# Ordering two sets of small matmuls by an empty GpSimd instruction instead of a TensorE drain, with another step moved between them

## The chip, the cores and the metric

The kernel runs on one core of a Trainium2 chip. The metric is the device time of one execution in microseconds; the time of a kernel is the median of its runs. A core has five engines that work side by side, each through its own queue in order: TensorE (PE in the profile; its weight loads are PEld), VectorE (DVE), ScalarE (ACT), GpSimd (POOL) and SyncE (SP, which here only starts transfers).

## The reference, cut to what matters

The first half is a recurrence per batch and head (4 batches, 8 heads, 768 steps, width 48); its result goes through a small three-way network:

```
cur = einsum('bhd,bhe->bhde', u * kt, vt)
y[:, :, t] = einsum('bhd,bhde->bhe', rt, state + cur)
state = wt[..., None] * state + einsum('bhd,bhe->bhde', kt, vt)
...
h = max(x @ w1, x @ w2, x @ w3);  out = h @ w_out
```

Here x holds y of all heads side by side: 3,072 tokens of 384 values, a hidden width of 768, all in float32.

## The kernel before, in words

The recurrence is worked out in 24 chunks of 128 steps (k = 0 to 23, six for each batch). For a chunk, scores of keys against receptances are a masked 128x128 matrix per head, and the values are taken with it; what came before the chunk enters through a carried state. On TensorE a chunk consists of short blocks of small matmuls, each named by a letter in a table of steps:

- R (`from_state`, L450): reads the carried state into the result y of the chunk.
- X (`scores`, L417): scores of a chunk, here of the next one, k + 1, into two `gram` banks.
- V and Z (`values` and `values2`, L489): two sets of 8 matmuls each that add scores times values into y. Z writes the same banks as V, from the other half of the array's rows.
- U (`to_state`, L460): keys times values for the next state. It uses all 128 rows of the array and is left out in the last chunk of a batch (k = 5, 11, 17, 23).
- T (L437): four transposes. R is left out in the first chunk of a batch.

All float32 matmuls show as two records each, with two weight loads. R, X, V and Z use the array as separate pieces of up to 64 rows and 64 columns; the network's matmuls (L147 and L167), T and U use all rows.

Between V and Z the function `values` puts `nc.tensor.drain()` (L482), an instruction of TensorE's own queue that holds it until the engine is empty.

The step letters stand in strings (`FRONT`, `LAST`, `TURN`, `ORD`); a "|" ends a unit, and units of the recurrence alternate with groups of the network's matmuls by a fixed rule. `ORD` sets chunks 4 to 23: its first unit is R, X of k + 1, V, U, Z, and E (`result`, L503: ScalarE copies y to x), and then b2 and d2, work on chunk k + 2. From chunk 8 on, d is two products on GpSimd (L373 and L374, here called the kr products), whose result VectorE sums into cs in step e (L387, three units later); e also lets GpSimd fill the matrix a with two selects (L393), and then M on VectorE (L426) puts the scores into a. V and Z read a.

Of the kernel before, what the change touches and what calls it, by code (L numbers as in the profile page):

```python
# [40 lines left out]
B, H, S, D = 4, 8, 768, 48  # L41
DM, FF = 384, 768
NP = 4
C = 128
# [7 lines left out]
HC = C // 2  # L52
CPH = HT // C
# [14 lines left out]
FRONT = "n2 w U0 b1 | d1 f1 r1 | w e1 c1 S0 W4 X1 T1 | R0 M0 | V0 Z0 E0 |"  # L68
LAST = "R0 M0 | V0 Z0 E0 n2 w U0 W9 n3 | b1 d1 | f1 r1 w | e1 c1 S0 X1 T1 R1 |"
TURN = "b1 d1 w | f1 w | r1 c1 | e1 M0 w | "  # L70
ORD = "w R0 X1 V0 U0 Z0 E0 b2 d2 | f2 n3 w | S0 r2 c2 | e2 M1 w | T1 w | |"


START = ("aaaaaaaaaaaacaaacaccaxmcacmcamcamcamcamcamcamcamcaamca"
# [16 lines left out]
def kernel(ctx: ExitStack, tc, tin, nat, u_flat, u_pair, v_t, w_all, out, ytr):  # L91
    nc = tc.nc
# [83 lines left out]
    with ExitStack() as fast:  # L176
# [21 lines left out]
        natt = {}  # L198
# [268 lines left out]
        def state(k):  # L467

            if goes_on(k):
                new = prep[k]["pu"][0:112, 0:NP * D].rearrange("p (a b) -> p a b", a=NP)  # L470
                if k % NCH > 0 and k >= CPH:
# [3 lines left out]
                nc.vector.tensor_tensor(out=sstar[(k + 1) % 2][0:112, :, 0:D], in0=new,  # L475
                                        in1=dec[(k + 1) % 2][0:112, :].unsqueeze(2).broadcast_to([112, NP, D]), op=ALU.mult)

        def values(k, second=False):
            p = prep[k]
            fresh = k % NCH == 0 and not second  # L480
            if second:
                nc.tensor.drain()  # L482
            for late in range(2):
                for row in range(2):
                    for half, m in ((0, 64), (1, 48)):
                        hh, j = row ^ second, (1 - row) ^ late
                        h, lo = 4 * half + 2 * j + hh, 64 * row
                        a = p["a"][lo:lo + HC, 2 * hh + half]
                        nc.tensor.matmul(p["y"][64 * half:64 * half + m, hh, j, HC * late:C],  # L489
                                         lhsT=natt[k][0][lo:lo + HC, h * D:h * D + m],  # L490
                                         rhs=a[:, j, :] if late else a[:, j::2 - j, :],
                                         start=fresh and not late, stop=True, skip_group_check=True)

        def values2(k):
            values(k, True)

        def result(k):
# [7 lines left out]
            for lo in (0, 64) if slot == CPH - 1 else ():  # L505
                for j in range(KT):
                    eng = nc.scalar if lo and half < PLAIN else nc.sync
                    eng.dma_start(out=x[lo + 48:lo + 64, j, :], in_=x[lo + 16 * j:lo + 16 * j + 16, KT, :])

        steps = dict(X=scores, M=take, T=transposes, R=from_state, U=to_state, S=state, V=values, Z=values2, E=result, n=load,  # L510
                     b=prep_scan_b, f=prep_scan_f, r=prep_rk, c=prep_check, d=prep_diag1, e=prep_diag2)
        ready = {("n", k) for k in range(3)}
# [16 lines left out]
        def attn():  # L529
            for step in "bdfeWrXTcW":  # L530
                ahead(step, 0) if step != "W" else warmer(2 if ("X", 0) in ready else 8)
            for k in range(NK):
                if k == CPH:
                    nc.scalar.dma_start(out=u_bc[:, :], in_=u_flat.partition_broadcast(128))
                for step in (FRONT if k < CPH - 1 else LAST if k < CPH else TURN + ORD if k == CPH else ORD).split():
                    if step == "|":
# [134 lines left out]
    with tc.If(verdict[0] != 0, label="general"), ExitStack() as slow:  # L671
# [9 lines left out]
        with tc.For_i(0, B) as b:  # L681
            for pr in range(NP):
# [18 lines left out]
                for j in range(KT):  # L701
                    with tc.For_i(0, 16) as i:
# [16 lines left out]
                        for q in range(2):  # L719
                            z = ps_z.tile([2, S // 2], F32, name="z")  # L720
                            nc.tensor.matmul(z[:, :], lhsT=sel[0:112, :], rhs=kv[0:112, q * (S // 2):(q + 1) * (S // 2)],
                                             start=True, stop=True)
                            nc.vector.tensor_copy(out=yo[:, q * (S // 2):(q + 1) * (S // 2)], in_=z[:, :])
                        for hh in range(2):
                            place, lo = 2 * hh + pr % 2, 64 * (pr // 2)
# [8 lines left out]
        for i in range(NW if w_all.dtype != F32 else 0):  # L734
# [3 lines left out]
            lo, hi = words[:, :, 0], words[:, :, 1]  # L738
# [93 lines left out]
```

## Time and profile before

| | |
|---|---|
| median of 3 runs | 424.89 us (424.53 to 431.61) |
| profiled execution, own time | 423.95 us |
| its span | 422.2 us |
| TensorE busy | 408.9 us, 97% of the span |
| VectorE, ScalarE, GpSimd busy | 272.0, 151.9, 74.3 us |
| drains on TensorE | 24, one per chunk |

The span runs from the first to the last instruction of the profiled execution; 1.75 us of its time lie around it. A matmul's end in the trace is modelled from its size, and matmuls overlap, so a block's length is read best from the start of one block to the start of the next.

### The profile page before, as it was taken

Reading aid. Unit: us, or ns where it says so; the run is one execution under the profiler, and the core shown is the slowest. Engines: PE = TensorE matmul, PEld = TensorE weight load, DVE = VectorE, ACT = ScalarE, POOL = GpSimd, SP = SyncE. Lnnn points to the kernel's source line nnn. Section 1 sums busy time; section 2 is a strip of 40 time slices with the busy share of each in tenths; the row PEclk is TensorE's granted clock in tenths of the full one; section 3 lists DMA queues with packets and bytes.
Section 4 is the critical chain, followed back from the end, with each engine's and each line's share of the span. In section 5 each row is a group of like instructions: output and inputs, shape, how many; then the busy total and the mean of one; then the engine's idle time right before and its main releaser. Section 6 shows DMA issues by size and latency. Waiting matters only on the chain.

```text
span 422.2 us, 9012 instructions
## 1 busy us (share of the span) xinstructions
PE 408.9 (97%) x3695; PEld 320.9 (76%) x3695; DVE 272.0 (64%) x515; ACT 151.9 (36%) x318; POOL 74.3 (18%) x92
## 2 busy tenths in 40 slices
PE   6989999999999999999999999999999999999995
PEld 3665545556678888987888988888988888988895
DVE  5988789877769977835867658658547624223320
ACT  1334344232554443424425455334523221312111
POOL 3120111030443140313023113113113100000000
PEclk9989999999999999999999999999999999999999
DMA  8835975244172403295735496653280000200002
GB/s 224 258 100 151 351 250 168 68 168 124 44 231 67 123 7 118 48 283 173 219 92 182 114 279 209 198 180 94 52 265 23 2 2 0 79 18 0 1 2 78
DMA packets 20702, 53.27 MB, mean 126 GB/s; under 512 B 2816, under 2 KB 9088, under 8 KB 20656
## 3 DMA queue, kind: packets, MB, share of 16 engines
q1 hardware_dynamic: 16832, 42.61, 33.3%
q10 hardware_dynamic: 3824, 10.03, 7.6%
q8 instruction: 30, 0.49, 0.5%
q14 instruction: 16, 0.13, 0.1%
HBM read 46.74 MB, written 4.72 MB: 122 GB/s over the span
## 4 chain that ended last, share of the span: by engine, by line
PE 92%; DVE 4%; issue 1%; DMA 1%; ACT 1%; POOL 0%; POOLq 0%; DVEq 0%; ACTq 0%
PE psm L147 55%; PE psm L167 17%; PE y L489 5%; PE gram L417 4%; PE y L450 3%; PE tu L460 3%; PE psm L526 2%; PE tu L437 2%; PE psm L383 1%; DMA out_dram<-m 1%; DVE tin L356 1%; DVE tin L357 1%; DVE gf L345 1%; DVE gf L335 1%; DVE x_lo L107 0%
## 5 line engine op out<-in xcount | busy, mean ns | idle before, releaser
L147 PE MATMUL psm<-x_hi,w 128*128 128x512 f32 x540 | 172.9, 394 | 0.6 <-ACT m L126 0.6
L147 PEld LDWEIGHTS psm<-x_hi,w 128*128 128x128 f32 x540 | 101.4, 188 | 22.5 <-ACT m L126 0.8
L147 PE MATMUL psm<-x_lo,w 128*128 128x512 f32 x270 | 105.3, 390 | 0.0
L129 DVE TENSOR_TENSOR m<-psm,m 128x512 f32<-128x512 f32 x60 | 41.2, 687 | 58.6 <-PE psm L147 52.6
L167 PE MATMUL psm<-w,h_hi 128*128 128x384 f32 x288 | 78.0, 364 | 0.0
L393 POOL TENSOR_SCALAR_AFFINE_SELECT a<-cs 64x512 f32<-64x512 f32 x48 | 35.5, 739 | 233.7 <-DVE cs L387 117.2
L147 PEld LDWEIGHTS psm<-x_lo,w 128*128 128x128 f32 x270 | 50.7, 188 | 9.9
L167 PEld LDWEIGHTS psm<-w,h_hi 128*128 128x128 f32 x288 | 51.8, 188 | 6.4
L147 PE MATMUL psm<-x,w 128*128 128x512 f32 x108 | 48.3, 598 | 0.0
L503 ACT COPY x<-y 112x512 f32<-112x512 f32 x24 | 14.1, 587 | 74.4 <-PE y L489 74.0
L167 PE MATMUL psm<-w,h_lo 128*128 128x384 f32 x120 | 40.2, 335 | 0.0
L362 ACT ACTIVATE gf<-gf 112x1034 f32<-112x1034 f32 x24 | 25.7, 1070 | 36.3 <-DVE tin L357 33.0
L106 ACT CAST h_hi<-m 128x512 fp32r<-128x512 f32 x30 | 18.7, 622 | 54.6 <-DVE m L129 54.6
L335 DVE TENSOR_TENSOR_SCAN gf<-tin,d_bwd 112x517 f32<-112x517 f32 x24 | 31.1, 1296 | 10.0 <-DMA tin<-in_tin_dram 10.0
L147 PEld LDWEIGHTS psm<-x,w 128*128 128x128 f32 x108 | 19.9, 190 | 22.8 <-issue 22.1
L107 DVE TENSOR_TENSOR h_lo<-m,h_hi 128x512 fp32r<-128x512 f32 x30 | 22.2, 740 | 19.0 <-ACT h_hi L106 19.0
L345 DVE TENSOR_TENSOR_SCAN gf<-tin,d_fwd 112x517 f32<-112x517 f32 x24 | 29.6, 1235 | 0.8
L489 PE MATMUL y<-a,v 64*64 64x128 f32 (+3 forms) x768 | 25.5, 248 | 2.9
L489 PEld LDWEIGHTS y<-a,v 64*64 64x64 f32 (+1 forms) x768 | 20.5, 126 | 6.0 <-issue 5.9
L373 POOL TENSOR_TENSOR kr<-kr 128x384 f32<-128x384 f32 x16 | 18.7, 1170 | 26.8 <-DMA kr<-in_nat_dram 25.8
L426 DVE COPY_PREDICATED a<-mask,gram 128x384 f32<-128x384 int32 x44 | 23.2, 582 | 0.0
L126 ACT COPY m<-psm 128x512 f32<-128x512 f32 x30 | 17.5, 582 | 15.9 <-PE psm L147 13.6
(71 smaller groups left out, 427.9 us busy)
## 6 DMA issues: line engine op xcount, KB each, us to landing
tin<-in_tin_dram SPq DMA_DIRECT2D x23, 677.7 KB, 5.5
w<-in_w_all_dram SPq DMA_DIRECT2D x24, 384.0 KB, 6.6
cv<-in_w_all_dram ACTq DMA_DIRECT2D x24, 384.0 KB, 3.3
kr<-in_nat_dram SPq DMA_DIRECT2D x16, 384.0 KB, 5.9
v<-in_nat_dram SPq DMA_DIRECT2D x24, 192.0 KB, 5.5
out_dram<-m SPq DMA_DIRECT2D x24, 192.0 KB, 2.3
x<-x SPq DMA_DIRECT2D x33, 32.0 KB, 2.0
tin<-in_tin_dram SPq DMA_DIRECT2D x1, 258.0 KB, 4.8
```

What stands on the lines that cost most here:

```text
L106: nc.scalar.copy(out=hi, in_=src)
L107: rest = lambda: nc.vector.tensor_tensor(out=lo, in0=src, in1=hi.bitcast(F32), op=ALU.subtract)
L129: nc.vector.tensor_tensor(out=m[:, :], in0=ps[:, :], in1=m[:, :], op=ALU.max)
L147: nc.tensor.matmul(ps[:, :], lhsT=wt[f * 3 + wi][:, ct * 128:(ct + 1) * 128], rhs=xt[:, ct, :], start=(n == 0), stop=(n == KT * len(terms) ...
L167: nc.tensor.matmul(pss[tt][:, 0:DM], lhsT=ht[f][:, tok], rhs=wt[FT * 3 + f][:, :], start=(f == 0 and i == 0), stop=(f == FT - 1 and i == l ...
L335: nc.vector.tensor_tensor_scan(out=gf[0:112, 0, ::-1], data0=t[0:112, 0:WC][:, ::-1], data1=d_bwd[0:112, ::-1], initial=0.0, op0=ALU.mult, ...
L345: nc.vector.tensor_tensor_scan(out=gf[0:112, 1, :], data0=tbuf[k % NB][0:112, 0:WC], data1=d_fwd[0:112, :], initial=0.0, op0=ALU.mult, op1 ...
L362: nc.scalar.activation(out=flat, in_=flat, func=AF.Square, accum_out=acc[0:112, k:k + 1])
L373: nc.gpsimd.tensor_tensor(out=n[:, 0, :], in0=n[:, 0, :], in1=n[:, 1, :], op=ALU.mult)
L393: nc.gpsimd.affine_select(out=a[rows, :, 0:2, :], pattern=[[0, 4], [0, 2], [1, HC]], in_=cs[rows, :].rearrange("p (a b) -> p a b", b=2).un ...
L426: nc.vector.copy_predicated(out=p["a"][:, 2 * hh:2 * hh + 2, :, :].rearrange("p a b c -> p a (b c)"), mask=mask_b(2), data=p["gs"][hh].rea ...
L489: nc.tensor.matmul(p["y"][64 * half:64 * half + m, hh, j, HC * late:C], lhsT=natt[k][0][lo:lo + HC, h * D:h * D + m], rhs=a[:, j, :] if la ...
```

## The change

For chunks 4 to 23 the drain goes. In its place stands an empty instruction on GpSimd (`nop`) that waits for the last matmul of V, and the first matmul of Z waits for that empty instruction. Chunks 0 to 3 keep the drain. In `ORD` the step X1 moves from ahead of V to between U and Z.

```
-ORD = "w R0 X1 V0 U0 Z0 E0 b2 d2 | f2 n3 w | S0 r2 c2 | e2 M1 w | T1 w | |"
+ORD = "w R0 V0 U0 X1 Z0 E0 b2 d2 | f2 n3 w | S0 r2 c2 | e2 M1 w | T1 w | |"
...
+        def after(later, sooner):
+            how = mybir.DependencyInfo(mybir.DependencyClass.Sync, mybir.DependencyReason.DATA)
+            tc.add_manual_dep(later.ins, sooner.ins.name, how, reason="the second values use the first's banks")
+            return later
...
-            if second:
+            if second and k < CPH:
                 nc.tensor.drain()
...
-                        nc.tensor.matmul(p["y"][64 * half:64 * half + m, hh, j, HC * late:C],
+                        mm = nc.tensor.matmul(p["y"][64 * half:64 * half + m, hh, j, HC * late:C],
...
+                        if "first" in p:
+                            after(mm, p.pop("first"))
+            if not second and k >= CPH:
+                p["first"] = after(nc.gpsimd.nop(nofuse=True), mm)
```

On TensorE, a chunk with R and U before the change. In these rows `y<-tin,sstar` (L450) is R, `gram` X, `y<-a,v` V and Z, `tu<-v,kn` U; the drain itself is not printed.

```order
L450 MATMUL y<-tin_114,sstar_136 48x128 x2
L417 MATMUL gram<-tin_115 64x2x64 [waits DMAHW7_49]
...
L417 MATMUL gram<-tin_115 64x64 x4
L489 MATMUL y<-a,v 64x128 [waits Pool_49]
...
L489 MATMUL y<-a,v 48x64
L460 MATMUL tu<-v,kn 64x48 [waits Activation_49]
...
L460 MATMUL tu<-v,kn 48x48
L489 MATMUL y<-a,v 64x128
L489 MATMUL y<-a,v 48x128
```

The same place after the change (V and Z now have line 495):

```order
L450 MATMUL y<-tin_114,sstar_136 48x128 x2
L495 MATMUL y<-a,v 64x128 [waits DMAHW7_49,Pool_49]
...
L495 MATMUL y<-a,v 48x64
L460 MATMUL tu<-v,kn 64x48 [waits Activation_49]
...
L460 MATMUL tu<-v,kn 48x48
L417 MATMUL gram<-tin_115 64x2x64 [waits DMAHW7_49]
...
L417 MATMUL gram<-tin_115 64x64 x4
L495 MATMUL y<-a,v 64x128 [waits Pool_sequencer_49]
```

X has moved behind U, and the first matmul of Z waits for GpSimd's own sequencer; there are 20 such waits, one for each of chunks 4 to 23.

On GpSimd, the stretch from the selects of one chunk to those of the next, before and after. The empty instruction is not printed; the wait on PE that it brings stands with the row behind it.

```order
 L393 AFFINE_SELECT a<-cs 64x4x128 [waits DVE_49,PE_49]
 L393 AFFINE_SELECT a<-cs 64x4x128 [waits Pool_49]
-L373 TENSOR_TENSOR kr<-kr 128x384 [waits DMAHW6_49,Pool_49]
+L373 TENSOR_TENSOR kr<-kr 128x384 [waits PE_49,DMAHW6_49,Pool_49]
 L374 TENSOR_TENSOR kr<-kr,u_bc 128x384 [waits Pool_49]
```

The empty instruction stands behind the selects and ahead of the kr products, so these are now queued behind V.

## Rows read from the trace of the kernel before

**Rows 1.** The page: span, TensorE's busy time, engines of the chain that ended last.

```profile
span 422.2 us, 9012 instructions
...
PE 408.9 (97%) x3695; PEld 320.9 (76%) x3695; DVE 272.0 (64%) x515; ACT 151.9 (36%) x318; POOL 74.3 (18%) x92
...
PE 92%; DVE 4%; issue 1%; DMA 1%; ACT 1%; POOL 0%; POOLq 0%; DVEq 0%; ACTq 0%
```

**Rows 2.** All waits of PE from 60 us on: total us, times, longest.

```profile
PE psm L147 <- ACT m L126: 0.6, 1, 0.6
PE tu L608 <- DVE good L606: 0.2, 1, 0.2
```

**Rows 3.** Timeline of PE, chunk 13: start, length, block.

```profile
201.29 0.66 PE L450 MATMUL y<-tin,sstar 48*64 48x128 f32 x16
201.78 0.83 PE L417 MATMUL gram<-tin 48*64 48x128 f32 x32
202.45 0.50 PE L489 MATMUL y<-a,v 64*48 64x128 f32 x16
202.88 0.67 PE L460 MATMUL tu<-v,kn 128*64 128x48 f32 x16
203.67 0.56 PE L489 MATMUL y<-a,v 64*64 64x128 f32 x16
204.16 0.50 PE L147 MATMUL psm<-x_hi,w 128*128 128x512 f32 x1
```

**Rows 4.** Timeline of PE, the network's matmul ahead of that chunk.

```profile
200.97 0.39 PE L147 MATMUL psm<-x_hi,w 128*128 128x512 f32 x1
```

**Rows 5.** Groups by line on PE: all of U, its 20 chunks.

```profile
L460 PE MATMUL tu<-v,kn 128*64 128x48 f32 (+1 forms) x320 | 13.3, 219 | 0.2 <-ACT kn L439 0.2
```

**Rows 6.** Timeline of PE, chunk 12, without R: X directly behind the network's matmuls.

```profile
185.08 0.90 PE L417 MATMUL gram<-tin 48*64 48x128 f32 x32
185.79 0.51 PE L489 MATMUL y<-a,v 64*48 64x128 f32 x16
```

**Rows 7.** Timeline of PE, chunk 11, without U: V, then Z.

```profile
171.43 0.50 PE L489 MATMUL y<-a,v 64*48 64x128 f32 x16
172.05 0.56 PE L489 MATMUL y<-a,v 64*64 64x128 f32 x16
```

**Rows 8.** Timeline of PE, chunk 23, the last: V, then Z.

```profile
358.73 0.50 PE L489 MATMUL y<-a,v 64*64 64x128 f32 x16
359.36 0.56 PE L489 MATMUL y<-a,v 64*64 64x128 f32 x16
```

**Rows 9.** Timeline of ACT, DVE, POOL and PEld: four handings-over between engines.

```profile
204.30 0.59 ACT L503 COPY x<-y 112x512 f32<-112x512 f32 x1 [2.05 <-PE y L489]
195.78 0.55 DVE L387 TENSOR_REDUCE cs<-kr 128x8 f32<-128x384 f32 x1
196.46 0.66 POOL L393 TENSOR_SCALAR_AFFINE_SELECT a<-cs 64x512 f32<-64x512 f32 x1 [10.08 <-PE tu L437]
2.92 0.20 POOL L521 MEMSET warm<- 128x128 bf16 x1
3.17 0.13 PEld L526 LDWEIGHTS <-warm 128*128 128x128 bf16 x2 [3.17 <-POOL warm L521]
0.34 0.10 POOL L820 MEMSET const-float32-1.0<- 128x1 f32 x1
```

**Rows 10.** Timeline of POOL: the kr products ahead of chunk 19's V, and the slowest.

```profile
291.32 1.01 POOL L373 TENSOR_TENSOR kr<-kr 128x384 f32<-128x384 f32 x1
292.41 1.34 POOL L374 TENSOR_TENSOR kr<-kr,u_bc 128x384 f32<-128x384 f32 x1
121.11 2.00 POOL L373 TENSOR_TENSOR kr<-kr 128x384 f32<-128x384 f32 x1 [0.39 <-DMA kr<-in_nat_dram]
123.19 1.01 POOL L374 TENSOR_TENSOR kr<-kr,u_bc 128x384 f32<-128x384 f32 x1
```

**Rows 11.** Timeline: V of chunk 19, the sum that reads its kr products, V of chunk 20.

```profile
296.43 0.50 PE L489 MATMUL y<-a,v 64*48 64x128 f32 x16
299.80 0.55 DVE L387 TENSOR_REDUCE cs<-kr 128x8 f32<-128x384 f32 x1
300.26 1.08 DVE L426 COPY_PREDICATED a<-mask,gram 128x384 f32<-128x384 int32 x2
311.84 0.50 PE L489 MATMUL y<-a,v 64*48 64x128 f32 x16
```

**Rows 12.** Timeline of POOL, the selects that end closest ahead of a V (chunk 7).

```profile
105.98 2.40 POOL L393 TENSOR_SCALAR_AFFINE_SELECT a<-cs 64x512 f32<-64x512 f32 x2 [10.38 <-PE psm L167]
```

**Rows 13.** Timeline of PE: that V, of chunk 7.

```profile
108.63 0.50 PE L489 MATMUL y<-a,v 64*64 64x128 f32 x16
```

More of the change, by code (lines that the diff above doesn't have):

```diff
@@ L488, in values @@
                         a = p["a"][lo:lo + HC, 2 * hh + half]
-                        nc.tensor.matmul(p["y"][64 * half:64 * half + m, hh, j, HC * late:C],
-                                         lhsT=natt[k][0][lo:lo + HC, h * D:h * D + m],
-                                         rhs=a[:, j, :] if late else a[:, j::2 - j, :],
-                                         start=fresh and not late, stop=True, skip_group_check=True)
+                        mm = nc.tensor.matmul(p["y"][64 * half:64 * half + m, hh, j, HC * late:C],
+                                              lhsT=natt[k][0][lo:lo + HC, h * D:h * D + m],
+                                              rhs=a[:, j, :] if late else a[:, j::2 - j, :],
+                                              start=fresh and not late, stop=True, skip_group_check=True)
+                        if "first" in p:
+                            after(mm, p.pop("first"))
+            if not second and k >= CPH:
+                p["first"] = after(nc.gpsimd.nop(nofuse=True), mm)
         def values2(k):
```

## The prediction

> **What bounds the kernel now.** I read the page first. TensorE is busy for 408.9 of 422.2 us, and 92% of the chain that ended last is its own work [rows 1]. The view of waits then shows that from 60 us on it waited for another engine only twice, 0.8 us in all [rows 2]. So TensorE's own queue sets the time from the fifth chunk on, which is where the change applies, and each 0.1 us taken from or added to that queue in a chunk shows in the end nearly whole. Then the timeline of TensorE over one chunk [rows 3]. What is to be read there is not how long a block is but how its start lies to the modelled end of the block ahead (start plus length):
>
> - Between blocks that both use separate pieces of the array: X starts at 201.78, R ends at 201.95; V starts at 202.45, X ends at 202.61. Both start about 0.17 us ahead of the end.
> - Where one of the two uses all rows: U at 202.88 against V's end at 202.95, the network's matmul at 204.16 against Z's end at 204.23, and R at 201.29 against 201.36 for the network's matmul ahead [rows 3, 4]. All three start 0.07 us ahead of the end, in whichever direction the array changes.
> - Over the drain: Z starts at 203.67, U ends at 203.55. That is 0.12 us behind the end.
>
> **The drain in chunks with U.** U has 320 records, 16 for a chunk, so 20 chunks have it [rows 5]; without chunks 0 to 3, which keep the drain, 16 are left (k = 4 to 22 but for 5, 11 and 17). There U is now followed by X, a change from all rows to pieces. Row for row that is the same change as from the network's matmul to R, so X should start 0.07 us ahead of U's end where Z started 0.12 behind it: 0.19 us per chunk, 16 x 0.19 = **3.0 us**. The bounds: nothing, if the array is empty at this change in any case and the modelled ends mislead; or 0.29 us per chunk (0.12 + 0.17), if X could follow U as X follows R.
>
> The Trainium skill has a rule that speaks against the larger value: by "TensorEngine Tiling (Array Packing)", section Key Properties, changing the tiling mode drains the engine, so a drain next to such a change is paid once already. By that rule the sum below holds; without it this term would be 16 x 0.29 = 4.6 us. The trace agrees with it: -0.07 us at each of the three changes of mode against -0.17 us without one.
>
> **The order of X.** The other joints only change places. Before: R to X and X to V, both at -0.17. After: R to V and X to Z, of the same kind. The first block behind a change of rows or a drain takes longer: X needs 0.71 us to the next start behind the network's matmuls against 0.67 behind R [rows 3, 6], and Z is 0.56 us long where V is 0.50. X now pays this behind U, and Z no longer does: +0.05 and -0.06, so zero. Where X was the first block of a chunk (6, 12, 18), V is now. The later X is no loss: M, which reads it, comes three units later on VectorE (15.4 us from V to the next V in rows 11, M 3.8 us behind V there). X's inputs and its two banks have been free since the M before, for which V waited already.
>
> **The drain in chunks without U.** In chunk 11 V ends at 171.93 and Z starts at 172.05, again +0.12 [rows 7]. Now V is followed by X and X by Z, all pieces. One joint at +0.12 becomes one at -0.17, 0.29 us, and Z loses its slow start, 0.06: 0.35 us in each of chunks 5, 11 and 17, **1.0 us**. Bounds: zero, if the wait for GpSimd is not over in time (next step), and this 1.0.
>
> **The new wait, and what covers it.** Its path is TensorE to GpSimd, the empty instruction, GpSimd to TensorE. The trace has no such row. The nearest: ScalarE starts 0.07 us behind Z's end (204.23 to 204.30), GpSimd 0.13 us behind VectorE's sum (196.33 to 196.46), TensorE's weight load 0.05 us behind a GpSimd memset (3.12 to 3.17), and the smallest GpSimd instruction has 0.10 us [rows 9]. Together an estimate of 0.2 to 0.3 us; as ends I keep 0.1 us (one handing-over each way and nothing between) and 2.0 us, the longest single GpSimd instruction [rows 10]. The cover: with U, X starts 0.53 us behind V's end (-0.07 + 0.67 - 0.07) and takes 0.72, so Z is due 1.25 us behind V's end. Without U it is -0.17 + 0.67 = 0.50 us. Both hold 0.3 us, so the wait costs nothing there. In chunk 23 no scores are left to move, so nothing covers it: Z, now 0.13 us behind V's end [rows 8], comes 0.25 to 0.3 us behind it, a loss of **0.15 us**. This holds if GpSimd is free when V ends. The closest is chunk 7: selects end at 108.38, V at 109.13 [rows 12, 13].
>
> **What is queued behind the wait.** The kr products. Before, they ran as soon as their data was there, often ahead of V (291.32 against V at 296.43) [rows 10, 11]; now they start behind V. In chunk 19 that is about 296.93 + 0.15 = 297.08, and with 1.01 and 1.34 us and the gap between them they end at 299.5; VectorE's sum wants them at 299.80. Chunk 15 has the same slack, the others more. With the slowest pair (121.11 to 124.20, 3.1 us) the sum would be 0.4 us late, and M behind it on VectorE (300.26) too, but the V that needs this M comes 11.6 us after it (311.84) [rows 10, 11]. I take zero, hidden behind the network's matmuls; without that cover it would be below 1 us over two chunks.
>
> **The sum.** 3.0 + 1.0 - 0.15 = 3.9 us. The profiled execution (423.95 us) would take 420.05. The median of the runs is 0.94 us above it: 424.89 - 3.9 = **421.0 us**.
>
> **The rivals.**
>
> - *The wait takes the drain's place.* TensorE's queue might stand still at Z until the engine is empty, as at the drain. Then X to Z is at +0.12 and not -0.17, and Z keeps its slow start: -0.35 us against the 0.19 won, 16 x 0.16 = 2.6 us lost, zero in chunks 5, 11 and 17, and 0.15: 427.6 us. If only half of the chunks do so, about 424. For it: an unfinished wait is not in the trace of before. Against it: V waits for GpSimd and still starts 0.17 us ahead of X's end [rows 3], so a wait that is already met costs nothing, and by the cover this one is met. Chance 0.10.
> - *A slow GpSimd, slower than before.* The mechanism is the path over GpSimd taking c us. It decides from 1.25 us on; a chunk with U breaks even at 1.25 + 0.19 = 1.44 us, one without at 0.85, and 16 (c - 1.44) + 3 (c - 0.85) + (c - 0.13) reaches 8.5 us, 2%, at c = 1.7. At 2.0 us it gives 14 us more, 439 us. For it: GpSimd instructions of 2.0 us exist [rows 10], and its queue runs in order. Against it: those stand behind the empty instruction now, and selects that stand ahead end at least 0.75 us before V does. Chance 0.04.
> - *The change of rows is no drain.* X follows U at -0.17: 16 x 0.29 + 1.0 - 0.15 = 5.5 us, 419.4 us. Against it are the three joints at -0.07. Chance 0.08.
> - *It doesn't do what it says*, or other waits take up what is won: no difference, 424.9 us. Twenty waits on GpSimd are in the program; TensorE has hardly any wait that could swallow them. Chance 0.04.
>
> **How the numbers follow.** My forecast has 0.74, with 419.9 to 422.5 us as its own range (the 1.0 us without U at either bound, and some 0.4 us between runs as between the two lower ones shown). The whole range, **419.0 to 424.8 us**, takes in the third rival, most of the fourth and the half case of the first, and leaves out the rest, near 0.15. Measurement tells about 2%, 8.5 us, from no change: below 416.4 us nothing here leads, 0.02; above 433.4 only the slow GpSimd does, 0.04; within, 0.94.
>
> **What will show it.** In the timeline of TensorE, X should start 0.07 us ahead of U's end, and Z 0.17 ahead of X's, with Z 0.50 us long; in chunk 23 Z's start behind V's end is the whole path over GpSimd. No wait of PE on POOL should appear but there. The kr products should start some 0.15 us behind each V's end. I am wrong on the mechanism if Z starts behind X's end; on a size if U to X is not at -0.07 us; on the cover if V or the network's matmuls start to wait for VectorE.

## The result

Against the kernel before on the same chip the change takes 0.9877 of its time, with a 95% interval of 0.9835 to 0.992: 5.2 us less of 424.7, so 419.5, with 3.4 to 7.0 us less inside the interval. Runs in which TensorE was granted 1.2 GHz for some 20 us near 25 to 45 us are left out of the ratios; the profiles of the change and of all experiments but two (three memsets, VectorE) are of such runs, so the stretches compared below lie behind that, at the full 2.4 GHz.

The page after: span, busy time, the slices of the granted clock, the chain.

```profile
span 425.0 us, 9013 instructions
...
PE 412.9 (97%) x3695; PEld 326.4 (77%) x3695; DVE 277.3 (65%) x515; ACT 151.5 (36%) x318; POOL 74.7 (18%) x92
...
PEclk9955899999999999999999999999999999999999
...
PE 92%; DVE 4%; DMA 2%; ACT 1%; issue 0%; SPq 0%; DVEq 0%; ACTq 0%; POOLq 0%
```

TensorE still sets the time. Its timeline in chunk 13 after (start, length, block) answers to [rows 3, 4]:

```profile
205.64 0.39 PE L147 MATMUL psm<-x_hi,w 128*128 128x512 f32 x1
205.95 0.66 PE L450 MATMUL y<-tin,sstar 48*64 48x128 f32 x16
206.45 0.50 PE L495 MATMUL y<-a,v 64*48 64x128 f32 x16
206.88 0.67 PE L460 MATMUL tu<-v,kn 128*64 128x48 f32 x16
207.47 0.90 PE L417 MATMUL gram<-tin 48*64 48x128 f32 x32
208.19 0.51 PE L495 MATMUL y<-a,v 64*48 64x128 f32 x16
208.64 0.50 PE L147 MATMUL psm<-x_hi,w 128*128 128x512 f32 x1
```

U ends at 207.55 and X starts at 207.47, 0.08 us ahead by these rounded rows; unrounded it is 0.07 in each of the 16 chunks with U. X ends at 208.37, Z starts at 208.19, 0.18 ahead, and is 0.51 us long. From R to the network's matmul behind Z the chunk takes 2.69 us where it took 2.87 [rows 3].

Chunk 11, without U (V, X, Z, and the network), then chunk 23, where no X is left. They answer to [rows 7] and [rows 8]:

```profile
176.83 0.50 PE L495 MATMUL y<-a,v 64*48 64x128 f32 x16
177.16 0.84 PE L417 MATMUL gram<-tin 48*64 48x128 f32 x32
177.83 0.51 PE L495 MATMUL y<-a,v 64*48 64x128 f32 x16
178.27 0.44 PE L167 MATMUL psm<-w,h_hi 128*128 128x384 f32 x1
...
361.24 0.50 PE L495 MATMUL y<-a,v 64*48 64x128 f32 x16
361.89 0.56 PE L495 MATMUL y<-a,v 64*64 64x128 f32 x16
```

In chunk 11 both joints are at -0.17. In chunk 23 Z starts 0.15 us behind V's end (361.74): that is the whole path TensorE to GpSimd to TensorE, counted from V's modelled end, and 0.02 us more than the drain cost there.

On GpSimd the kr products of chunks 11 and 19 now stand behind V, and VectorE's work next to those of chunk 19 reads so:

```profile
177.62 1.03 POOL L373 TENSOR_TENSOR kr<-kr 128x384 f32<-128x384 f32 x1 [2.30 <-PE y L495]
...
299.92 1.00 POOL L373 TENSOR_TENSOR kr<-kr 128x384 f32<-128x384 f32 x1 [5.33 <-PE y L495]
301.00 1.01 POOL L374 TENSOR_TENSOR kr<-kr,u_bc 128x384 f32<-128x384 f32 x1
```

```profile
301.06 1.56 DVE L356 TENSOR_TENSOR tin<-tin,gf 112x256 f32<-112x256 f32 x2
...
303.42 0.54 DVE L387 TENSOR_REDUCE cs<-kr 128x8 f32<-128x384 f32 x1
```

The products end at 302.01, the sum that reads them starts at 303.42, so it isn't they that hold it. But two multiplications of VectorE that run beside them took 1.56 us, against 0.76 in the same chunk before; the last section has the check that it is the products that slow them.

### The profile page after: what moved, and what is told of

Read it like the earlier page. It is cut to its first block, busy times and chain, and to the rows that moved or that the text cites. A ratio compares the mean times of both kernels' runs of the same rounds, so it can differ in the third digit from the quotient of the medians.

```text
span 425.0 us, 9013 instructions
## 1 busy us (share of the span) xinstructions
PE 412.9 (97%) x3695; PEld 326.4 (77%) x3695; DVE 277.3 (65%) x515; ACT 151.5 (36%) x318; POOL 74.7 (18%) x92
## 4 chain that ended last, share of the span: by engine, by line
PE 92%; DVE 4%; DMA 2%; ACT 1%; issue 0%; SPq 0%; DVEq 0%; ACTq 0%; POOLq 0%
PE psm L147 55%; PE psm L167 17%; PE y L495 4%; PE gram L417 4%; PE y L450 3%; PE tu L460 3%; PE tu L437 2%; PE psm L536 1%; DMA tin<-in_tin_dram 1%; PE psm L383 1%; DVE gf L345 1%; DMA out_dram<-m 1%; DVE gf L335 1%; DVE tin L357 1%; DVE tin L356 1%; DVE kr L371 0%
## 5 line engine op out<-in xcount | busy, mean ns | idle before, releaser
L129 DVE TENSOR_TENSOR m<-psm,m 128x512 f32<-128x512 f32 x60 | 41.2, 688 | 55.8 <-PE psm L147 50.2
L373 POOL TENSOR_TENSOR kr<-kr 128x384 f32<-128x384 f32 x16 | 19.8, 1235 | 92.9 <-PE y L495 87.9
L345 DVE TENSOR_TENSOR_SCAN gf<-tin,d_fwd 112x517 f32<-112x517 f32 x24 | 34.4, 1432 | 0.8
L107 DVE TENSOR_TENSOR h_lo<-m,h_hi 128x512 fp32r<-128x512 f32 x30 | 20.7, 689 | 17.2 <-ACT h_hi L106 17.2
L495 PE MATMUL y<-a,v 64*48 64x128 f32 (+3 forms) x768 | 27.0, 260 | 0.6
L495 PEld LDWEIGHTS y<-a,v 64*64 64x64 f32 (+1 forms) x768 | 23.4, 136 | 3.8 <-issue 1.9
```

What stands on the lines that cost most here:

```text
L107: rest = lambda: nc.vector.tensor_tensor(out=lo, in0=src, in1=hi.bitcast(F32), op=ALU.subtract)
L129: nc.vector.tensor_tensor(out=m[:, :], in0=ps[:, :], in1=m[:, :], op=ALU.max)
L345: nc.vector.tensor_tensor_scan(out=gf[0:112, 1, :], data0=tbuf[k % NB][0:112, 0:WC], data1=d_fwd[0:112, :], initial=0.0, op0=ALU.mult, op1 ...
L373: nc.gpsimd.tensor_tensor(out=n[:, 0, :], in0=n[:, 0, :], in1=n[:, 1, :], op=ALU.mult)
L495: mm = nc.tensor.matmul(p["y"][64 * half:64 * half + m, hh, j, HC * late:C], lhsT=natt[k][0][lo:lo + HC, h * D:h * D + m], rhs=a[:, j, :] ...
```

## The experiments

**The change again**, unchanged, with more runs. 

> The changed kernel once more, timed in more rounds. My theory counts joints on TensorE: a block starts 0.12 us behind the modelled end of the block ahead where a drain lies between, 0.07 us ahead of it where the array changes between all rows and pieces, 0.17 us ahead of it between blocks in pieces. From the trace after: 16 chunks x 0.19 us + 3 chunks x 0.35 us - 0.03 us in chunk 23 (path over GpSimd 0.15 us) = 4.1 us less than before, a ratio of 0.990. The rival, that something outside these chunks changed too, would hold the ratio near the 0.9877 first measured, 5.2 us.

Ratio 0.9852, interval 0.9812 to 0.9891, 6.3 us less. The count of joints, 0.990, lies just outside, and by the test set ahead the rival came nearer: something outside these joints may differ too. This is taken up below.

**The hop without the move.** Against the change:

```
-ORD = "w R0 V0 U0 X1 Z0 E0 b2 d2 | ...
+ORD = "w R0 X1 V0 U0 Z0 E0 b2 d2 | ...
```

> The drain becomes the empty GpSimd instruction, but X stays ahead of V. My theory: U alone covers the path (Z is due 0.53 us behind V's end, the path takes 0.15 us), so Z starts 0.07 us ahead of U's end in 16 chunks, 3.0 us won; in chunks 5, 11, 17 and 23 Z starts 0.15 us behind V's end, where the drain had 0.12: 0.1 us lost. 2.9 us below before, ratio 0.993; so X between the sets is worth only the 1.1 us of three chunks. Rival: X is needed as a cover in every chunk, then Z starts behind U's end and the time is that of before.

Ratio 0.992, interval 0.988 to 0.9959; expected 0.993. Timeline of PE: U, Z and the network in a chunk with U, then V and Z of chunk 11.

```profile
164.67 0.67 PE L460 MATMUL tu<-v,kn 128*64 128x48 f32 x16
165.26 0.56 PE L495 MATMUL y<-a,v 64*64 64x128 f32 x16
165.75 0.50 PE L147 MATMUL psm<-x_hi,w 128*128 128x512 f32 x1
...
177.97 0.50 PE L495 MATMUL y<-a,v 64*48 64x128 f32 x16
178.62 0.56 PE L495 MATMUL y<-a,v 64*64 64x128 f32 x16 [0.15 <-POOLq L502]
```

Z starts 0.08 us ahead of U's end (165.34): U alone covers the path. In chunk 11, where nothing does, Z waits 0.15 us for GpSimd's sequencer. So the drain's replacement brings the larger part in all 16 chunks with U, and the move of X only what three chunks hold. The timing by itself doesn't tell this kernel from the change, whose interval overlaps this one. The stretch from chunk 4 to the last Z, compared under "The kernel before again", does: it runs from 71.33 to 363.99 us here, 3.0 to 3.1 us less than before and 1.1 to 1.2 more than with the change.

**The move without the hop.** The kernel before, with the step table of the change:

```
-ORD = "w R0 X1 V0 U0 Z0 E0 b2 d2 | ...
+ORD = "w R0 V0 U0 X1 Z0 E0 b2 d2 | ...
```

> The drain stays in all chunks, X moves between U and Z. My theory: U to X at -0.07 us, X to Z at +0.12 us, and both X and Z start slowly: 16 x 0.15 = 2.4 us slower than before, nothing in chunks 5, 11, 17 and 23; ratio 1.006. This is also the price that my first rival would have had. Rival: the new order itself brings part of the gain, then this is faster than before by 1 us or more.

Ratio 1.0028, interval 0.999 to 1.0065: not faster, and too small for the timing alone to tell from none. The timeline of PE tells it:

```profile
165.12 0.66 PE L450 MATMUL y<-tin,sstar 48*64 48x128 f32 x16
...
166.64 0.90 PE L417 MATMUL gram<-tin 48*64 48x128 f32 x32
167.66 0.56 PE L489 MATMUL y<-a,v 64*64 64x128 f32 x16
168.15 0.50 PE L147 MATMUL psm<-x_hi,w 128*128 128x512 f32 x1
```

X ends at 167.54, Z starts 0.12 us behind, and the chunk takes 3.03 us, 0.16 more than before. Over the whole stretch (71.57 to 371.25 us) it is 2.7 to 2.8 us more, where 2.4 was expected. So the order by itself costs; it pays only with the wait in place of the drain.

**U behind Z.** Against the change:

```
-ORD = "w R0 V0 U0 X1 Z0 E0 b2 d2 | ...
+ORD = "w R0 V0 X1 Z0 U0 E0 b2 d2 | ...
```

> A step further than the change: R, V, X, Z, U, with the empty GpSimd instruction kept. U stands between Z and the network's matmuls, so the array changes between pieces and all rows once less on each side of X. My theory, per chunk with U against the change: V to X at -0.17 instead of V to U at -0.07, no change ahead of X (-0.17 and no slow start, 0.10 + 0.05 less), U to the network's matmul at -0.16 as between T and those: about 0.24 us less in 16 chunks, 3.9 us below the change, ratio to before 0.981. X alone must cover the path over GpSimd: 0.50 us against 0.15. Rival: 0.50 us is not enough because TensorE's queue meets the wait too late, then Z starts behind X's end and the gain is gone; or the later U makes the carried state late and R waits.

Ratio 0.9834, interval 0.9796 to 0.9872, the fastest of all kernels here; in the same comparison the change had 0.9852, so the timing doesn't tell the two apart. Timeline of PE, one chunk:

```profile
163.67 0.66 PE L450 MATMUL y<-tin,sstar 48*64 48x128 f32 x16
164.16 0.50 PE L495 MATMUL y<-a,v 64*48 64x128 f32 x16
164.49 0.84 PE L417 MATMUL gram<-tin 48*64 48x128 f32 x32
165.16 0.51 PE L495 MATMUL y<-a,v 64*48 64x128 f32 x16
165.60 0.67 PE L460 MATMUL tu<-v,kn 128*64 128x48 f32 x16
166.19 0.50 PE L147 MATMUL psm<-x_hi,w 128*128 128x512 f32 x1
```

The chunk takes 2.52 us, 0.17 less than with the change, where I expected 0.24. X does cover the path (Z at -0.17). The miss is the last joint: U ends at 166.27 and the network starts at 166.19, -0.08 and not -0.16. U has all 128 rows but only 64 columns of the array (128*64), the network 128*128, and I read this as a change of layout too. That isn't shown apart: whatever follows U without a drain, in any of these traces, starts at -0.07, so it could also be U's own end. By these rows it is 16 x 0.17 = 2.7 us, by the stretch (73.02 to 363.44 us) 2.4 us less than with the change. R starts 0.07 us ahead of the network's end as before, so the later U makes nothing late.

**A longer path, three memsets.** Against the change; for the next run the loop has 7 turns:

```
-                p["first"] = after(nc.gpsimd.nop(nofuse=True), mm)
+                first = after(nc.gpsimd.memset(idle[:, :], 0.0), mm)
+                for _ in range(2):
+                    first = nc.gpsimd.memset(idle[:, :], 0.0)
+                p["first"] = first
```

> The changed kernel with a longer path over GpSimd: in place of the empty instruction three memsets of an unused 128x128 tile, one behind the other, the first waiting for V and the last released to Z. From the 0.20 us memset of that size in the trace before and the 0.15 us of the path as measured, I estimate a path of 0.8 to 1.0 us; it is read from chunk 23, where nothing covers it. My theory, cover 1.25 us with U and 0.50 us without: Z still starts 0.17 to 0.18 us ahead of X's end in all 16 chunks with U; in chunks 5, 11 and 17 it starts 0.3 to 0.5 us later than that of the change's -0.17. Rival, the cover is no more than the time from which TensorE's queue reaches the wait (some 0.4 us ahead, as its semaphore instructions stand in the trace): then Z is late with U too.

One run, 422.39 us. Timeline of PE, chunk 11 (V, X, Z) and chunk 23 (V, Z):

```profile
169.83 0.50 PE L496 MATMUL y<-a,v 64*48 64x128 f32 x16
170.16 0.84 PE L418 MATMUL gram<-tin 48*64 48x128 f32 x32
171.28 0.56 PE L496 MATMUL y<-a,v 64*64 64x128 f32 x16 [0.28 <-POOL idle L505]
...
355.88 0.50 PE L496 MATMUL y<-a,v 64*48 64x128 f32 x16
357.33 0.56 PE L496 MATMUL y<-a,v 64*64 64x128 f32 x16 [0.95 <-POOL idle L505]
```

The waits of PE on GpSimd from 60 us on (total us, times, longest):

```profile
PE y L496 <- POOL idle L505: 1.8, 4, 0.9
```

The path is 0.95 us. In chunk 11 Z is 0.28 + 0.17 = 0.45 us later than it would be without a wait: 0.95 - 0.50. There are four such waits, three chunks without U and the last; with U there is none, so the cover there holds 0.95 us and the rival is out.

**A longer path, eight memsets.** 

> The same with eight memsets: an estimated path c of 1.9 to 2.3 us, read from chunk 23. My theory: Z starts c - 1.25 us later than without in the 16 chunks with U, c - 0.50 in three, c - 0.15 in the last; at c = 2.1 that is 16 x 0.85 + 3 x 1.6 + 1.95 = 20 us over the change, some 15 us over before. Rival: TensorE drains on the wait itself and adds a further fixed gap to each, or the wait is partly hidden by later work, which would show in TensorE's idle time ahead of Z against c minus the cover.

One run, 454.7 us. Timeline of PE, Z in chunk 10 with U, in chunk 11 without, and in chunk 23:

```profile
173.48 0.56 PE L496 MATMUL y<-a,v 64*64 64x128 f32 x16 [0.83 <-POOL idle L505]
...
188.27 0.56 PE L496 MATMUL y<-a,v 64*64 64x128 f32 x16 [1.59 <-POOL idle L505]
...
387.52 0.56 PE L496 MATMUL y<-a,v 64*64 64x128 f32 x16 [2.25 <-POOL idle L505]
```

The path is 2.25 us. With U Z is 0.83 + 0.18 = 1.01 us late, so the cover is 1.24; without U 1.59 + 0.17 = 1.76, so it is 0.49. Both as worked out ahead, 1.25 and 0.50. An unmet wait costs the path less its cover and no fixed gap ahead of Z. Z itself is then a little slower, 0.48 us to the next start (173.48 to 173.96) against 0.45 in chunk 13 of the change. Over the stretch (71.77 to 388.01 us) it is 24.6 us more than with the change; the late Z explain 16 x 1.01 + 3 x 1.76 + 2.10 = 23.5 of them.

**The hop over VectorE.** Against the change:

```
-                p["first"] = after(nc.gpsimd.nop(nofuse=True), mm)
+                p["first"] = after(nc.vector.nop(nofuse=True), mm)
```

> The empty instruction stands in VectorE's queue and not in GpSimd's. VectorE mostly runs ahead of TensorE there (in chunk 13 before, the scan that stands behind V in the program started at 201.26, V at 202.45), so my theory: where it is ahead Z starts on time and VectorE itself stands still until V ends, up to some 2 us a chunk, which TensorE hardly feels; where it is behind with earlier work, Z waits for that. I expect Z late in a few chunks and 0 to 4 us over the change. Rival: any idle sequencer does as well, the time is that of the change and no Z is late.

One run, 421.2 us. The waits of PE, and the group of VectorE's scan that stands behind the empty instruction (busy us, mean ns, idle us before them and what ended it):

```profile
PE psm L147 <- ACT m L126: 1.4, 1, 1.4
...
PE y L495 <- DVEq L502: 0.2, 1, 0.2
```

```profile
L335 DVE TENSOR_TENSOR_SCAN gf<-tin,d_bwd 112x517 f32<-112x517 f32 x24 | 31.7, 1321 | 42.9 <-PE y L495 41.1 <-DMA tin<-in_tin_dram 1.7
```

TensorE waits for VectorE only in chunk 23, 0.16 us. My expectation of a few late Z was wrong and the rival right there. That the time is that of the change isn't shown: there is one run, and its stretch (63.03 to 356.43 us) is 0.5 to 0.6 us longer than the change's. That VectorE itself stands still was right: 41.1 us of its idle time end with V. Part of this it would have spent idle elsewhere (its idle time ahead of L129 is 40.4 us here and 55.8 with the change), and here it could afford the rest.

**The kernel before again.** 

> The kernel before, unchanged, to have its profile beside those of the others. My theory: from the first block of chunk 4 to the network's matmul behind the last Z the stretch is 296.2 us as in the first profile, give or take 1.3 us for the one wait on ScalarE near chunk 13, and the part ahead of chunk 4 is that of the change at an equal granted clock. Rival: the part ahead of chunk 4 is over 1 us longer here than with the change, which would explain why the measured ratio is larger than 16 x 0.19 + 3 x 0.35 us.

One run, 433.54 us. The stretch from the first block of chunk 4 to the network's matmul behind the last Z, busy us of each engine and the granted clock: first of this run, then of the change, then of the change again.

```profile
72.98:368.73 295.75, 293.20 (x2837) 235.71 (x2836) 204.56 (x379) 115.79 (x250) 63.25 (x68) 1.00 0.41 126
```

```profile
71.25:362.38 291.13, 290.98 (x2837) 235.38 (x2836) 209.29 (x379) 115.53 (x250) 63.90 (x68) 1.00 0.43 128
```

```profile
72.49:365.22 292.73, 291.26 (x2837) 235.40 (x2836) 210.40 (x379) 115.44 (x250) 62.83 (x68) 1.00 0.42 127
```

Of the 1.6 us between the two profiles of the change, the wait of [rows 2], near chunk 13, explains 1.55. It stands between T and the network's matmul; first of the change, then of the change again, then of the first profile of before:

```profile
201.38 0.55 PE L437 MATMUL tu<-ident,tin 112*128 112x112 f32 x4
201.70 0.47 PE L147 MATMUL psm<-x_hi,w 128*128 128x512 f32 x1
...
202.62 0.55 PE L437 MATMUL tu<-ident,tin 112*128 112x112 f32 x4
204.49 0.50 PE L147 MATMUL psm<-x_hi,w 128*128 128x512 f32 x1 [1.32 <-ACT m L126]
...
195.81 0.55 PE L437 MATMUL tu<-ident,tin 112*128 112x112 f32 x4
196.98 0.50 PE L147 MATMUL psm<-x_hi,w 128*128 128x512 f32 x1 [0.62 <-ACT m L126]
```

Without a wait, in the first pair, the network follows T's start by 0.32 us; in the others it is 1.87 and 1.17 us, and 0.66 in the second profile of before (205.13 to 205.79). So the wait costs more than the idle time printed with it: 1.55, 0.85 and 0.34 us. Without it the stretch is 295.3 and 295.4 us before (296.18 - 0.85 in the first profile, 63.66 to 359.84 us, and 295.75 - 0.34) and 291.1 and 291.2 us after: 4.1 to 4.3 us less, where the count of joints has 4.1. The stretches named with the other experiments are compared in the same way; there the wait cost 0.37 us (the hop), 1.53 (the move), 1.68 (U behind Z), 0.50 (eight memsets) and 1.68 (VectorE).

## Why the prediction was right

The forecast was 3.9 us less than before; the timing says 5.2 with 3.4 to 7.0 inside, and the stretch of the trace in which the change works 4.1 to 4.3 us. The time of 419.5 us lies in the whole range, but 1.5 us under the 421.0 forecast, just under the forecast's own range (from 419.9), and on the number of the third rival (419.4). The time alone would have pointed at that rival; what decides for the forecast is the joints. By its steps:

- **TensorE's queue sets the time.** Right: what left the queue came out at the end. In the stretch TensorE's idle time fell from 296.18 - 293.13 = 3.05 us to 291.13 - 290.98 = 0.15 us, the one exposed wait in chunk 23.
- **The drain next to U, 3.0 us.** Right: the joint went from +0.12 (0.10 in one chunk) to -0.07 in all 16, and the hop alone took 3.0 to 3.1 us off the stretch. That the change of layout still costs its share was decisive: -0.07 us at such a joint against -0.17 without, in every trace here. "TensorEngine Tiling (Array Packing)", Key Properties, of the Trainium skill says that changing the tiling mode drains the engine. The traces agree that a change of mode costs, but only in part: it costs 0.10 us, and a drain next to it a further 0.19, so it did not do all that the drain did. Read to the letter, with the engine just as empty at the change, the rule would have left nothing to win, the prediction's lower bound. So "paid once already" in the prediction holds for 0.10 of the 0.29 us; its sum took -0.07 from the rows and stands without the rule. The rival without the cost of a change (419.4 us from 424.9) is ruled out by the traces: X never followed U at -0.17.
- **The chunks without U, 1.0 us.** Right, shown by the change against the hop alone: -0.17 against +0.15 at that joint, and 1.1 to 1.2 us between the two stretches.
- **The order of X, zero.** Right with the wait. The run of the move alone shows the price if Z had still been held until the engine is empty: 0.16 us more per chunk, the first rival.
- **The cover, 1.25 and 0.50 us.** Right, 1.24 and 0.49 by the long paths. A path of 1.7 us would have been needed for a loss of 2%; 2.25 us did more than that.
- **The path, 0.2 to 0.3 us.** Too long: it is 0.15, so chunk 23 lost 0.02 us and not 0.15.
- **The kr products, zero.** Right in the end, but not in how. They start 0.29 us behind V's end (177.33 to 177.62 and 299.63 to 299.92), not 0.15. And I had not counted that they now run beside other work of VectorE: its busy time in the stretch rises from 204.6 to 209.3 us (204.63 and 204.56 in the two profiles of before). TensorE waited for none of it.

The measured gains, 5.2 and 6.3 us, are 1 to 2 us above the count of joints (16 x 0.19 + 3 x 0.35 - 0.02 = 4.1 us). The trace shows at most 0.2 us of that within the stretch. Some may be the wait on ScalarE, which cost from nothing to 1.55 us in the profiles of the two kernels, and some the parts around the stretch: it starts anywhere from 63.0 to 63.7 us in three profiles and from 71.3 to 73.0 in the other seven, with no order by kernel, and 62.3 to 63.5 us lie behind it (65.0 with eight memsets). No run here divides the rest, so its cause stays open: the mechanism is shown for the 4.1 us, not for the whole of what was timed.

## What to carry to other kernels

When one engine's queue is nearly full, read its timeline joint by joint: start of a block against the modelled end of the one ahead. A drain can be replaced by a wait that goes through another engine's sequencer, and such a wait is free for TensorE as long as the work put between the two ends outlasts its path. It isn't free for the other engine: what stands behind the wait in its queue is held as well, so choose an engine with time to spare. Put between the two ends work of the same array layout, and place the block with another layout where the layout changes least often; here that further step was worth 2.4 us in the trace, while the timing didn't tell it from the change.

## What the runs showed of the hardware

- These joints on TensorE were of one size in all ten profiles, from chunk 4 on: -0.16 to -0.18 us to the modelled end between blocks in pieces that wait for nothing, -0.07 where the layout changes, and +0.12 over a drain (0.10 to 0.18 in single chunks). Other joints without a change have other sizes, as the -0.23 from T to the network in chunk 13 above.
- From the modelled end of a matmul over GpSimd's empty instruction back to a matmul takes 0.15 us, over VectorE's 0.16 (one chunk). A GpSimd product queued behind the empty instruction starts at 0.29.
- Moving two GpSimd products in time cost VectorE time: the mean of its second scan rose from 1235 to 1432 ns. The groups of before and after:

```profile
L345 DVE TENSOR_TENSOR_SCAN gf<-tin,d_fwd 112x517 f32<-112x517 f32 x24 | 29.6, 1235 | 0.8
```

```profile
L345 DVE TENSOR_TENSOR_SCAN gf<-tin,d_fwd 112x517 f32<-112x517 f32 x24 | 34.4, 1432 | 0.8
```

  The runs in which the products aren't held behind V, the move alone and the hop over VectorE, have 1235 ns again; the hop alone, which holds them without moving X, has 1381. So it is the products, not the new order.
